# Attention with a distance bias and two feed-forward stages: rows 64 to 191 of the bias built by distance, scores of full pairs from three fp32r products

## The chip, the cores and the metric

One core of a Trainium2 chip. The metric is the device time of one execution in microseconds (us); 585.6 us is the median of three runs of the kernel before (585.51 to 585.66). In this kernel and at this scatter a difference under about 0.2% (1.2 us) can't be told from none.

## The reference

```python
B, H, S, D = 2, 8, 576, 64
scores = q @ k.T / 8
x = log1p(|i - j|) / log1p(max(i, 1))
bias = relu(x * w1 + b1) @ w2                  # 32 hidden units, 8 heads
attn = softmax(scores + bias) @ v              # then 1152 tokens x 512
h = x @ w_in;   g = P(h) / Q(h);  y = g @ w_out      # 512 -> 2048 -> 512, rational function
h = y @ w2_in;  z = piecewise quadratic of h;  out = z @ w2_out
```

The bias depends on the row i and on the distance |i - j|. All is fp32.

## The kernel before, in words

**Order.** Every operation of the attention stage is registered under a kind and a number (`op`, L179), with the letters of the engines that may run it: P TensorE (PE), V VectorE (DVE), A ScalarE (ACT), G GpSimd (POOL), S the DMA queue of SyncE (SP). The table `PLAN` (L34) gives each a position and one letter; `run` (L769) sorts the positions and issues in that order. Each engine works through its own instructions in this order, so an instruction that waits holds back all behind it on its engine. The first steps of the feed-forward stage (`gen`) and the splits of its first weights (`w00` to `w14`, six of the input and seven of the output weights) stand in the same table; the rest of that stage follows in its own loop (`moe`, L624).

**Bias** (`bias_rows`, L251). 36 blocks of 16 rows. A block has four `relu` (L271 to L274, 128 partitions = 4 rows x 32 units), matmuls against w2 (`mm`, L285), a scaled eviction from PSUM (`bev`, L288) and a `st` store. Blocks 0 to 11 (rows 0 to 191) are "near": all 576 columns, each half in its own PSUM bank (or, for those in `one`, both halves in one double bank), stored into an SBUF tile `bias0`. Later blocks are functions of the distance: they compute only max(576 - i0, i0 + 16) distances, mirror the rest (`mir`, L300), go to DRAM (`bd`), and a load per unit and head (`lb`, L326) reads each row at its own shift into one of four `bias` tiles. `dup` (L486) copies rows 0 to 63 to the upper partitions.

**Attention** (`attn`, L345). 20 units: five row blocks ("t": rows 0 to 63 of both batches together, then 0 to 3: 128 rows each from row 64) times four head pairs; 36 pairs of work, 4 of "t" and 32 full ones. A pair is scores (`qk`, L372: fp32 matmuls, per 288 columns one on rows 0 to 63 of the array for the even head and one on rows 64 to 127 for the odd), `ttr` (L397, DVE: add the bias, take the row's extreme), `exp` (L402, ACT, with row sum), `eps` (L406: add 1e-9 to two sums), `rec` (L410), `norm` (L213), nine transposes (`tr`, L431), three evictions (`tev`), 20 matmuls with V (`pv`, L446), and `xh`/`xl` (L463, L465), which split the result into an fp32r part and an fp32r remainder for the next stage. K stays in SBUF as fp32 (`lk`, L489), Q is loaded per unit (`lq`).

**Feed-forward.** Each product is three fp32r matmuls (high x high, high x low, low x high; L714 and L757), 12 of 384 columns per step; ACT, DVE and POOL do the functions between.

Of the kernel before, what the change touches and what calls it, by code (L numbers as in the profile page):

```python
# [31 lines left out]
PAR = {'pb': 4, 'ptb': 3, 'ahead': 2, 'hid': 9, 'bbuf': 6, 'drg': 1.764, 'vb': 4, 'hb': 4, 'qb': 4, 'gb': 11, 'lag': 9, 'shift': 3, 'inb': 4, 'outb': 3, 'c2': 2, 'c3': 1, 's0': [1, 1, 2, 3, 4, 4], 's1': [1, 2, 3], 'mp': 4.15, 'cw': [10, 12, 14, 16], 'cl': [[0, 3, 6, 9], [5, 8, 11, 14]], 'bias': 4, 'one': [0, 1, 2, 3, 4, 8, 5, 9], 'early': 8, 'load': [1.69, 1.22, 0.773]}  # L32

PLAN = {  # L34
    'us0': ([0],
# [25 lines left out]
    'exp': ([98, 100, 132, 135, 173, 175, 182, 218, 217, 216, 238, 235, 279, 263, 293, 323, 316, 335, 336, 367, 357, 358, 402, 408, 450, 442, 454, 482, 486, 490, 519, 520, 553, 549, 574, 587, 588, 607, 622, 611, 670, 688, 693, 692, 707, 699, 708, 745, 763, 764, 769, 779, 817, 819, 844, 846, 881, 883, 902, 903, 922, 934, 955, 954, 968, 960, 970, 999, 998, 1003, 1014, 1027],
        'AAAAAAAAAAAAAAAAAAAAAAAAAAAAAAAAAAAAAAAAAAAAAAAAAAAAAAAAAAAAAAAAAAAAAAAA'),
    'eps': ([102, 137, 176, 219, 237, 241, 280, 325, 337, 380, 375, 434, 456, 487, 516, 552, 554, 589, 617, 654, 689, 694, 710, 760, 788, 787, 820, 878, 906, 905, 937, 957, 969, 1001, 1026, 1028],
        'AAAAAAAAAAAAAAAAAAAAAAAAAAAAAAAAAAAA'),
# [2 lines left out]
    'rec': ([120, 159, 185, 231, 239, 244, 300, 332, 347, 381, 379, 438, 468, 492, 517, 556, 559, 602, 618, 659, 690, 701, 738, 762, 789, 808, 826, 888, 907, 913, 941, 958, 983, 1012, 1033, 1029],
        'VVVVVVVVVVVVVVVVVVVVVVVVVVVVVVVVVVVV'),
    'norm': ([147, 146, 165, 164, 189, 188, 236, 247, 254, 252, 255, 253, 301, 303, 350, 345, 365, 364, 383, 382, 426, 425, 440, 461, 470, 471, 496, 502, 530, 528, 561, 558, 581, 560, 605, 604, 627, 661, 668, 669, 721, 718, 720, 719, 765, 739, 773, 771, 803, 798, 827, 828, 850, 851, 889, 891, 908, 910, 914, 929, 946, 976, 959, 971, 987, 1000, 1020, 1019, 1038, 1041, 1042, 1030],
        'GGGGGGAGGGAGGGGVGGGGGVGGVGGAGGGVGGGGGGGGGGGGAVGGGAGGGGGGAVGVVGAVGAGAGAAA'),  # L70
    'mir': ({12: 151, 13: 187, 14: 201, 15: 260, 16: 313, 17: 296, 18: 339, 19: 340, 20: 361, 21: 506, 22: 412, 23: 453, 24: 501, 25: 258, 26: 529, 27: 570, 28: 579, 29: 623, 30: 527, 31: 731, 32: 625, 33: 772, 34: 744, 35: 709},
        'GGGAAGAAAGGAAGGVAAAAGGGA'),
    'tr': ([153, 156, 157, 170, 169, 168, 193, 194, 192, 249, 257, 248, 262, 287, 285, 256, 283, 304, 305, 330, 306, 351, 353, 352, 370, 371, 372, 401, 428, 430, 429, 444, 432, 462, 463, 464, 474, 476, 475, 514, 534, 535, 540, 545, 550, 571, 569, 568, 592, 593, 591, 651, 650, 649, 653, 663, 662, 676, 677, 675, 722, 733, 732, 723, 727, 724, 784, 786, 778, 776, 785, 777, 805, 804, 806, 829, 831, 830, 852, 873, 853, 898, 899, 900, 919, 920, 928, 938, 939, 940, 952, 978, 977, 994, 993, 992, 1007, 1006, 1008, 1023, 1024, 1025, 1046, 1047, 1051, 1048, 1050, 1049],
        'PPPPPPPPPPPPPPPPPPPPPPPPPPPPPPPPPPPPPPPPPPPPPPPPPPPPPPPPPPPPPPPPPPPPPPPPPPPPPPPPPPPPPPPPPPPPPPPPPPPPPPPPPPPP'),
# [2 lines left out]
    'lv': ([197, 198, 202, 200, 204, 203, 270, 268],
        'SSSSSSSS'),
    'pv': ([205, 228, 251, 302, 355, 329, 354, 369, 427, 473, 472, 513, 512, 562, 578, 590, 648, 674, 717, 716, 774, 775, 832, 799, 884, 897, 896, 926, 951, 962, 1004, 1044, 1043, 1045, 1068, 1067],
        'PPPPPPPPPPPPPPPPPPPPPPPPPPPPPPPPPPPP'),  # L80
    'xh': ({0: 240, 2: 277, 4: 317, 6: 326, 8: 377, 10: 447, 12: 489, 14: 526, 16: 597, 18: 687, 20: 697, 22: 780, 24: 792, 25: 847, 26: 849, 27: 818, 28: 904, 29: 909, 30: 935, 31: 975, 32: 991, 34: 1055, 36: 1057, 38: 1079},
# [821 lines left out]
```

## Time and profile before

| | us |
|---|---|
| median of the runs | 585.6 |
| the profiled execution | 586.15 |
| its span, first to last instruction | 584.3 |
| PE busy | 568.4 (97%) |
| DVE busy | 482.1 (83%) |
| ACT busy | 416.0 (71%) |
| POOL busy | 328.6 (56%) |

Rows name line, engine, operation, output<-input. A busy PE may hold several matmuls in flight, so its busy time says that it had work, not that it ran at its peak; the chain of waits says whether others waited for it. PE, LD (PEld, weight loads), DVE, ACT and POOL run side by side. The granted TensorE clock is 1.00 in every stretch, the upper of its two levels (2.4 GHz).

### The profile page before, as it was taken

The numbers are of one execution on the slowest core, as the hardware profiler recorded it, in microseconds if no ns is written. First come the engines' busy times: TensorE is split into PE (matmuls) and PEld (weight loads), VectorE is DVE, ScalarE is ACT, GpSimd is POOL, SyncE is SP. The second block draws the span as 40 slices with busy tenths as digits, with TensorE's granted clock in tenths as the row PEclk, the third lists the DMA queues.
The fourth block names the chain that finished last, engine by engine and source line by source line (L and its number), as shares of the span: only waits on it lengthen the run. The fifth ranks groups of instructions, "written<-read, shape, count | busy, mean of one in ns | idle before, by whom it ended". The sixth has DMA issues, their size and how long they took to land.

```text
span 584.3 us, 11340 instructions
## 1 busy us (share of the span) xinstructions
PE 568.4 (97%) x4164; PEld 514.7 (88%) x4164; DVE 482.1 (83%) x951; ACT 416.0 (71%) x912; POOL 328.6 (56%) x335
## 2 busy tenths in 40 slices
PE   5999999999999899999999999999999999999997
PEld 3466766678788899999999999999999999999997
DVE  6998788889979888989998979999985998784332
ACT  5999999998999988787888788356554554443430
POOL 0343223343358776899998876664761964574220
PEclk9999999999999999999999999999999999999999
DMA  6985545575712112222221212331431222100012
GB/s 222 226 284 168 188 134 189 191 221 186 253 49 108 37 54 92 73 73 81 101 73 72 73 37 72 109 108 38 145 108 37 98 83 73 38 36 1 29 48 88
DMA packets 25288, 62.72 MB, mean 107 GB/s; under 512 B 3601, under 2 KB 7569, under 8 KB 25233
## 3 DMA queue, kind: packets, MB, share of 16 engines
q1 hardware_dynamic: 25088, 61.90, 32.3%
q8 instruction: 33, 0.54, 0.4%
q14 instruction: 23, 0.18, 0.1%
q10 hardware_dynamic: 144, 0.10, 0.1%
HBM read 48.83 MB, written 9.62 MB: 100 GB/s over the span
## 4 chain that ended last, share of the span: by engine, by line
PE 85%; ACT 6%; DVE 6%; issue 2%; DMA 1%; DVEq 0%; ACTq 0%
PE outps L757 31%; PE inps L714 31%; PE vps L446 7%; PE tps L431 6%; PE sps L382 6%; PE bps L285 4%; ACT P L402 1%; ACT hid L272 1%; DVE wc L522 1%; DVE x2l L690 1%; DVE wc L526 1%; DVE hid L274 1%; DMA small<-small 1%; ACT v L581 1%; ACT h L579 1%
## 5 line engine op out<-in xcount | busy, mean ns | idle before, releaser
L757 PE MATMUL outps<-gh,wo 128*128 128x384 f32 x768 | 209.5, 335 | 0.0
L620 POOL TENSOR_TENSOR gl<-v,gh 128x384 fp32r<-128x384 f32 x96 | 110.8, 1155 | 78.6 <-ACT gh L616 74.2
L757 PEld LDWEIGHTS outps<-gh,wo 128*128 128x128 f32 x768 | 139.9, 188 | 0.0
L757 PE MATMUL outps<-gl,wo 128*128 128x384 f32 x384 | 128.3, 334 | 0.0
L714 PE MATMUL inps<-x,wh 128*128 128x384 f32 x384 | 99.0, 338 | 1.8 <-DVE v L612 1.7
L213 POOL TENSOR_SCALAR P<-P,m 128x576 f32<-128x576 f32 x51 | 38.2, 757 | 71.7 <-DVE m L410 60.0
L583 ACT ACTIVATE v<-inps,cst 128x384 f32<-128x384 f32 x48 | 27.8, 579 | 66.5 <-PE inps L714 63.6
L714 PEld LDWEIGHTS inps<-x,wh 128*128 128x128 f32 x384 | 69.0, 188 | 3.8 <-DVE v L612 3.4
L757 PEld LDWEIGHTS outps<-gl,wo 128*128 128x128 f32 x384 | 72.1, 188 | 0.0
L607 DVE SCALAR_TENSOR_TENSOR v<-v 128x384 f32<-128x384 f32 x48 | 39.5, 823 | 34.1 <-ACT v L583 33.9
L714 PE MATMUL inps<-x2l,wh 128*128 128x384 f32 x192 | 64.6, 337 | 1.7 <-DVE x2l L690 1.7
L616 ACT ACTIVATE gh<-v 128x384 fp32r<-128x384 f32 x96 | 50.8, 529 | 20.4 <-DVE v L608 19.3
L714 PE MATMUL inps<-x2h,wh 128*128 128x384 f32 x192 | 64.6, 337 | 0.0
L714 PE MATMUL inps<-x,wl 128*128 128x384 f32 x192 | 64.5, 336 | 0.0
L714 PE MATMUL inps<-x2h,wl 128*128 128x384 f32 x192 | 64.5, 336 | 0.0
L526 DVE SCALAR_TENSOR_TENSOR wc<-raw,wc 128x512 int32<-128x512 int32 x64 | 59.4, 937 | 0.1
L587 POOL TENSOR_TENSOR q<-h,q 128x384 f32<-128x384 f32 x48 | 49.4, 1031 | 16.3 <-ACT q L580 15.9
L397 DVE CUSTOM_DVE_ANT_0 P<-sps,bias 128x576 f32<-128x576 f32 x72 | 51.9, 752 | 7.4 <-PE sps L382 3.4
L402 ACT ACTIVATE P<-P,m 128x576 f32<-128x576 f32 x72 | 55.2, 768 | 2.7 <-DVE m L397 2.7
L579 ACT ACTIVATE h<-inps,sb 128x384 f32<-128x384 f32 x48 | 28.3, 589 | 29.1 <-PE inps L714 29.1
L672 DVE TENSOR_TENSOR acc<-acc,outps 128x384 f32<-128x384 f32 x61 | 33.4, 547 | 18.8 <-PE outps L757 18.8
L446 PEld LDWEIGHTS vps<-PT,V 128*64 128x64 f32 x800 | 39.5, 137 | 7.6 <-issue 4.1
(83 smaller groups left out, 1211.3 us busy)
## 6 DMA issues: line engine op xcount, KB each, us to landing
raw<-w SPq DMA_DIRECT2D x64, 512.0 KB
bd<-bbuf SPq DMA_DIRECT2D x24, 295.5 KB
bias<-bd SPq DMA_DIRECT2D x24, 288.0 KB
bias<-bbuf SPq DMA_DIRECT2D x12, 288.0 KB
V<-v SPq DMA_DIRECT2D x8, 320.0 KB
K<-kc SPq DMA_DIRECT2D x4, 576.0 KB
out<-acc SPq DMA_DIRECT2D x12, 192.0 KB
Q<-qm SPq DMA_DIRECT2D x16, 128.0 KB
```

The lines of the kernel that those rows point to most:

```text
L213: nc.gpsimd.tensor_scalar(out, x, scale, 1.0, ALU.mult, ALU.mult)
L382: PE.matmul(S_[2 * i + e][c:c + w, x, :288], lhsT=Q[n][r, bb, 0:w], rhs=f(K[hp])[r, bb, 288 * x:288 * x + 288], start=True, stop=True, til ...
L397: V.tensor_tensor_reduce(halves(o), S_.pop(t)[:, :, :288], halves(bt), -0.125, 3e38, ALU.add, ALU.min, sums[i][:, 0, e:e + 1])
L402: A.activation(s, s, AF.Exp, bias=m[:, 0, e:e + 1], scale=-1.0, accum_out=m[:, 1, e:e + 1])
L446: PE.matmul(out[64 * e:64 * e + 64], lhsT=Vt[hp][:, bb, j, 64 * e:64 * e + 64], rhs=PT[i][:, (j, 5 + j if j < 4 else 4)[e], c], start=(j = ...
L526: return [(dict(V=0.7), lambda e: V.scalar_tensor_tensor(tc, words[:, :, 0], 29, tc, ALU.logical_shift_right, ALU.bitwise_or))]
L587: return [lambda: G.tensor_tensor(o["q"], o["h2"], o["q"], ALU.add)] if m == 0 else []
L607: return [lambda: V.scalar_tensor_tensor(v, v, 1.0, v, ALU.min, ALU.mult), lambda: V.tensor_tensor(v, v, h2, ALU.add)]
L616: return [lambda: A.activation(gh, o["v"], AF.Copy)]
L620: return [lambda: G.tensor_tensor(gl, o["v"], f(o["gh"]), ALU.subtract)]
L714: nc.tensor.matmul(ps[:, :U], lhsT=w[:, c], rhs=y[:, c], start=(t == 0), stop=(t == 11))
L757: nc.tensor.matmul(ps[:, :U], lhsT=w[:, c], rhs=y, start=(t == 0), stop=(t == 11))
```

## The change

1. Blocks 4 to 11 (rows 64 to 191) become like the later ones: 512 down to 400 distances instead of 576 columns, one bank, a mirror, a store to DRAM, and loads for units 4 to 7 (8 more `lb`, 8 more `mir`, 8 fewer `mm` and 4 fewer `bev`). One `bias0` tile is left, for "t".
2. Full pairs (not "t"): K and Q are split into fp32r high and low parts (`kh`, `kl`, `qh`, `ql`), and scores are the sum of three fp32r products, the two heads in turn. The high and low K parts take all eight slots of the ring in which four K and the first split output weights (`wo`) lay before. Raw K of two head pairs is held in tiles that later take `x`, of the others in the near pool.
3. `eps`, `dup`, `xh` may go to more engines; raw Q has 3 buffers, split Q 3, `hid` 10; the table is new.

Letters of the table that differ (before -> after): relu A 61, V 83 -> A 71, V 73; bev A 25, V 19 -> A 23, V 17; mir A 12, G 11, V 1 -> A 7, G 20, V 5; eps A 36 -> A 15, V 7, G 14; xh A 24 -> A 9, V 15; tev A 59, V 49 -> A 68, V 40; norm A 12, V 9, G 51 -> A 9, V 10, G 53; w03 A 1, V 2, G 3 -> V 1, G 5; w04 G 6 -> V 4, G 2; w13 V 2, G 5 -> A 1, V 1, G 5; w14 V 3, G 4 -> V 4, G 3. New: kh A 2, V 1, G 1; kl V 3, G 1; qh A 7, G 8, V 1; ql V 2, G 14. Of these, kh of head pairs 0 to 2, kl of 0 to 2, qh and ql of the first unit and the mirrors of blocks 4 to 11 stand ahead of the `ttr` of the first full pair.

```diff
-PAR = {... 'hid': 9, ... 'one': [0, 1, 2, 3, 4, 8, 5, 9], ...}
+PAR = {... 'hid': 10, 'q': 3, 'qs': 3, ... 'one': [0, 1, 2, 3], ...}
...
 def near_row(pr, m):
-    return 64 * (pr // 4) + pr % 4 + 4 * m
+    return pr + 4 * m
...
-        near = pr < 12
+        near = pr < 4
...
-                b = 64 * (pr >= 8)
-                nc.sync.dma_start(self.bias0[pr >= 4][b + pr % 4:b + 64:4], st["buf"][:, 0:S])
+                nc.sync.dma_start(self.bias0[pr:64:4], st["buf"][:, 0:S])
...
+        def split_q(e, n, low):
+            if low:
+                Ql[n] = self.slot(pq, "Ql", cfg["qs"], [128, B, 128], F32R)
+                self.sub(e, Ql[n], Q[n], f(Qh[n]))
+            else:
+                Qh[n] = self.slot(pq, "Qh", cfg["qs"], [128, B, 128], F32R)
+                self.copy(e, Qh[n], Q[n])
+
+        def load_k(hp):
+            K[hp] = f(self.xs0(hp, "Kx")[:, 0:3]).rearrange("p a c -> p (a c)") if hp < 2 else self.kn[hp - 2]
+            nc.sync.dma_start(K[hp], a["kc"][hp])
+
+        def split_k(e, hp, low):
+            x = K[hp]
+            if low:
+                Kl[hp] = self.ring("Kl")
+                self.sub(e, Kl[hp], x, f(Kh[hp]))
+            else:
+                Kh[hp] = self.ring("Kh")
+                self.copy(e, Kh[hp], x)
...
-                        PE.matmul(S_[2 * i + e][c:c + w, x, :288], lhsT=Q[n][r, bb, 0:w],
-                                  rhs=f(K[hp])[r, bb, 288 * x:288 * x + 288], start=True, stop=True,
-                                  tile_position=(64 * e, c))
+                    for m, (q, y) in enumerate(((Qh[n], Kh[hp]), (Qh[n], Kl[hp]), (Ql[n], Kh[hp]))):
+                        for e in range(2):
+                            r = slice(64 * e, 64 * e + 64)
+                            PE.matmul(S_[2 * i + e][c:c + w, x, :288], lhsT=q[r, bb, 0:w], rhs=y[r, k],
+                                      start=m == 0, stop=m == 2, tile_position=(64 * e, c))
...
-                bt = self.bias0[bk == 0][:, h] if bk in (0, "t") else bias[n, e][:]
+                bt = self.bias0[:, h] if bk == "t" else bias[n][:, e]
...
-            bias[n, e] = self.load_bias(pq, bk, h, cfg["bias"])
+            if n not in bias:
+                bias[n] = self.slot(pq, "bias", 2, [128, B, S])
+            self.load_bias(bias[n][:, e], bk, h)
...
-            for e in range(2) if n >= 8 else ():
+            if n >= 4:
+                op("qh", n, "VAG", lambda e, n=n: split_q(e, n, 0))
+                op("ql", n, "VG", lambda e, n=n: split_q(e, n, 1))
+            for e in range(2) if n >= 4 else ():
```

## Rows read from the trace of the kernel before

**Rows 1.** Windows: us, busy of PE, PEld, DVE, ACT, POOL (instructions), clock, DMA

```profile
15.00:45.00 30.00, 29.31 (x373) 15.77 (x367) 28.49 (x76) 29.66 (x68) 12.93 (x20) 1.00 0.86 246
45.00:142.00 97.00, 96.48 (x1068) 68.08 (x1063) 83.60 (x236) 92.56 (x239) 33.78 (x49) 1.00 0.57 187
142.00:197.00 55.00, 53.08 (x469) 45.33 (x468) 48.54 (x112) 51.10 (x120) 31.74 (x34) 1.00 0.36 119
5.00:45.00 40.00, 37.13 (x453) 20.64 (x455) 37.69 (x98) 37.05 (x78) 12.93 (x20) 1.00 0.84 250
```

**Rows 2.** Chain of waits: start, us, what; one full pair, the ramp, feed-forward

```profile
58.44 1.17 PE sps L382 x8
59.61 1.13 PE tps L431 x9
...
188.31 0.47 ACT q L580
...
197.59 2.09 PE outps L757 x12
...
300.06 2.08 PE inps L714 x12
```

**Rows 3.** Timeline of PE and PEld in one pair's scores: start, us, engine, line

```profile
130.73 0.41 PE L382 MATMUL sps<-K,Q 64*128 64x288 f32 x2
130.73 0.19 PEld L382 LDWEIGHTS sps<-K,Q 64*128 64x128 f32 x2
130.97 0.41 PE L382 MATMUL sps<-K,Q 64*128 64x288 f32 x2
```

**Rows 4.** Groups by line and form, PE: busy us, mean ns | idle before

```profile
L285 PE MATMUL bps<-hid,w2s 128*32 128x288 f32 x208 | 17.2, 451 | 7.7 <-DVE hid L274 6.6 <-ACT bbuf L201 0.7
...
L285 PE MATMUL bps<-hid,w2s 128*32 128x512 f32 x8 | 1.0, 592 | 0.0
...
L285 PE MATMUL bps<-hid,w2s 128*32 128x400 f32 x8 | 0.9, 511 | 0.0
```

**Rows 5.** Groups by line and form, ACT

```profile
L272 ACT ACTIVATE hid<-us,thr 128x576 f32<-128x576 f32 x15 | 11.1, 770 | 3.4 <-DVE thr L243 3.0 <-PE bps L285 0.3
L406 ACT ACTIVATE m<-m,cst 128x2 f32<-128x2 f32 x36 | 10.2, 289 | 0.3
...
L463 ACT ACTIVATE x<-vps 128x256 fp32r<-128x256 f32 x12 | 4.5, 376 | 0.1
...
L201 ACT ACTIVATE bbuf<-bps,small 128x288 f32<-128x288 f32 x4 | 1.9, 485 | 0.0
...
L201 ACT ACTIVATE wh<-wc 128x512 fp32r<-128x512 f32 x2 | 1.3, 630 | 0.0
...
L201 ACT ACTIVATE bbuf<-bps,small 128x448 f32<-128x448 f32 x1 | 0.6, 623 | 0.0
```

**Rows 6.** Groups by line and form, DVE

```profile
L205 DVE COPY PT<-tps 128x384 f32<-128x384 f32 x49 | 26.1, 549 | 6.7 <-PE tps L431 6.4
L274 DVE TENSOR_SCALAR hid<-us,thr 128x576 f32<-128x576 f32 x33 | 15.5, 529 | 0.9 <-PE bps L285 0.7
...
L216 DVE TENSOR_TENSOR wl<-wc,wh 128x512 fp32r<-128x512 f32 x5 | 5.0, 1009 | 0.0
...
L205 DVE CAST wh<-wc 128x512 fp32r<-128x512 f32 x7 | 5.0, 709 | 0.0
...
L274 DVE TENSOR_SCALAR hid<-u,thr 128x464 f32<-128x464 f32 x2 | 0.9, 446 | 0.0
```

**Rows 7.** Groups by line and form, POOL

```profile
L216 POOL TENSOR_TENSOR wl<-wc,wh 128x512 fp32r<-128x512 f32 x27 | 38.2, 1418 | 6.1 <-DVE wh L205 3.2 <-ACT wh L201 2.9
...
L211 POOL TENSOR_SCALAR wh<-wc 128x512 fp32r<-128x512 f32 x23 | 15.5, 674 | 25.1 <-PE inps L714 22.7 <-DVE wc L526 2.5
```

**Rows 8.** Timeline of DVE and POOL while POOL was idle, early

```profile
10.59 7.18 DVE L274 TENSOR_SCALAR hid<-us,thr 128x576 f32<-128x576 f32 x16 [0.44 <-PE bps L285]
...
19.51 2.94 POOL L486 COPY bias<-bias 64x576 f32<-64x576 f32 x4 [18.58 <-DMA bias<-bbuf]
```

More of the change, by code (lines that the diff above doesn't have):

```diff
@@ L29, in f @@
     return ap.bitcast(F32)
-PAR = {'pb': 4, 'ptb': 3, 'ahead': 2, 'hid': 9, 'bbuf': 6, 'drg': 1.764, 'vb': 4, 'hb': 4, 'qb': 4, 'gb': 11, 'lag': 9, 'shift': 3, 'inb': 4, 'outb': 3, 'c2': 2, 'c3': 1, 's0': [1, 1, 2, 3, 4, 4], 's1': [1, 2, 3], 'mp': 4.15, 'cw': [10, 12, 14, 16], 'cl': [[0, 3, 6, 9], [5, 8, 11, 14]], 'bias': 4, 'one': [0, 1, 2, 3, 4, 8, 5, 9], 'early': 8, 'load': [1.69, 1.22, 0.773]}
+PAR = {'pb': 4, 'ptb': 3, 'ahead': 2, 'hid': 10, 'q': 3, 'qs': 3, 'bbuf': 6, 'drg': 1.764, 'vb': 4, 'hb': 4, 'qb': 4, 'gb': 11, 'lag': 9, 'shift': 3, 'inb': 4, 'outb': 3, 'c2': 2, 'c3': 1, 's0': [1, 1, 2, 3, 4, 4], 's1': [1, 2, 3], 'mp': 4.15, 'cw': [10, 12, 14, 16], 'cl': [[0, 3, 6, 9], [5, 8, 11, 14]], 'bias': 4, 'one': [0, 1, 2, 3], 'early': 8, 'load': [1.69, 1.22, 0.773]}
@@ L61 @@
[L61 to L64, printed above, removed]
@@ L65 @@
-    'late': ([110],
-        'S'),
[L67 to L74, printed above, removed]
@@ L77 @@
[L77 to L81, printed above, removed]
-        'AAAAAAAAAAAAAAAAAAAAAAAA'),
@@ L91 @@
-    'w00': ([455, 596, 705, 797, 836, 1031],
-        'AAAAAA'),
-    'w01': ([478, 615, 740, 807, 842, 1058],
-        'VVVVVV'),
-    'w02': ([481, 619, 758, 887, 894, 1060],
-        'VVVVVV'),
-    'ab': ([504],
-        'S'),
-    'w03': ([533, 626, 770, 890, 924, 1061],
-        'VGVGAG'),
-    'w04': ([580, 796, 795, 1040, 925, 1086],
-        'GGGGGG'),
-    'bias_end': ([813],
-        '-'),
-    'lw1': ([814, 815, 855, 859, 862, 867, 869, 870, 871],
-        'SSSSSSSSS'),
-    'w10': ([837, 848, 916, 948, 1002, 1063, 1064],
-        'AAAAAAA'),
@@ L109 @@
[L109 to L119 removed]
+    'kh': ([122, 18, 63, 291],
+        'AVAG'),
+    'ql': ({4: 19, 5: 234, 6: 300, 7: 337, 8: 430, 9: 490, 10: 529, 11: 538, 12: 612, 13: 686, 14: 744, 15: 791, 16: 857, 17: 932, 18: 949, 19: 984},
+        'VGGGGGGGGGVGGGGG'),
@@ new lines @@
+    'lv': ([164, 165, 212, 214, 213, 61, 219, 221],
+        'SSSSSSSS'),
+    'mir': ({4: 64, 5: 123, 6: 113, 7: 111, 8: 76, 9: 115, 10: 112, 11: 128, 12: 247, 13: 281, 14: 184, 15: 270, 16: 266, 17: 323, 18: 338, 19: 359, 20: 364, 21: 482, 22: 489, 23: 546, 24: 532, 25: 297, 26: 533, 27: 610, 28: 611, 29: 695, 30: 552, 31: 761, 32: 746, 33: 788, 34: 805, 35: 745},
+        'AAGGVGGAAAGGGGGVGGGAGGGGGGVVGGAV'),
+    'dup': ([72, 91, 110, 108, 107, 109, 114, 160],
+        'GGGGGGGG'),
+    'qk': ([89, 103, 138, 157, 167, 228, 255, 277, 308, 328, 352, 391, 447, 471, 505, 510, 540, 562, 589, 628, 666, 698, 707, 711, 758, 782, 840, 847, 888, 914, 944, 947, 985, 990, 1007, 1044],
+        'PPPPPPPPPPPPPPPPPPPPPPPPPPPPPPPPPPPP'),
@@ new lines @@
+    'ttr': ([92, 93, 116, 117, 139, 140, 168, 169, 207, 211, 237, 238, 260, 267, 285, 301, 311, 325, 341, 342, 370, 396, 424, 425, 454, 455, 474, 476, 511, 512, 516, 517, 569, 570, 590, 591, 602, 603, 655, 656, 681, 688, 713, 714, 727, 734, 739, 740, 766, 768, 828, 829, 841, 842, 870, 871, 910, 912, 923, 924, 952, 959, 967, 968, 991, 992, 1008, 1010, 1034, 1038, 1045, 1046],
+        'VVVVVVVVVVVVVVVVVVVVVVVVVVVVVVVVVVVVVVVVVVVVVVVVVVVVVVVVVVVVVVVVVVVVVVVV'),
+    'kl': ([145, 194, 118, 320],
+        'VVVG'),
@@ new lines @@
+    'exp': ([120, 126, 127, 148, 154, 189, 197, 196, 208, 244, 264, 249, 274, 279, 332, 333, 335, 334, 373, 395, 381, 408, 436, 438, 466, 468, 475, 488, 521, 523, 534, 551, 596, 572, 608, 615, 625, 677, 670, 674, 691, 722, 730, 726, 728, 756, 748, 773, 811, 830, 853, 849, 863, 864, 879, 874, 920, 925, 941, 940, 961, 960, 974, 975, 994, 998, 1014, 1029, 1047, 1048, 1064, 1063],
+        'AAAAAAAAAAAAAAAAAAAAAAAAAAAAAAAAAAAAAAAAAAAAAAAAAAAAAAAAAAAAAAAAAAAAAAAA'),
+    'eps': ([147, 150, 195, 224, 245, 265, 296, 339, 344, 405, 417, 439, 469, 492, 530, 581, 609, 620, 678, 683, 733, 749, 783, 774, 833, 856, 868, 887, 938, 942, 962, 976, 1015, 1050, 1049, 1069],
+        'GVAGVGGGAAGVAGGGAVAGVGAVVGAAAAAAAAGG'),
@@ new lines @@
+    'rec': ([149, 175, 199, 236, 250, 268, 307, 360, 346, 406, 419, 444, 486, 514, 553, 582, 622, 654, 689, 684, 736, 760, 787, 812, 835, 859, 882, 911, 953, 964, 969, 996, 1018, 1051, 1052, 1071],
+        'VVVVVVVVVVVVVVVVVVVVVVVVVVVVVVVVVVVV'),
+    'norm': ([162, 161, 182, 183, 225, 231, 252, 253, 259, 258, 269, 302, 319, 318, 362, 361, 363, 358, 421, 410, 431, 420, 484, 481, 491, 493, 531, 528, 554, 555, 585, 584, 649, 650, 661, 662, 690, 697, 687, 696, 750, 747, 770, 775, 789, 790, 815, 813, 836, 855, 872, 869, 883, 931, 926, 922, 955, 954, 971, 970, 983, 982, 1002, 1000, 1028, 1023, 1058, 1060, 1097, 1084, 1073, 1083],
+        'GGGGGGGGGGVVGGGGGVGAGGGGGGGGGGGGGGGGAGGGGGVAGGVGGGGAVGGGGVGGGGVAAAVVAAGG'),
@@ new lines @@
+    'tev': ([185, 186, 190, 205, 210, 209, 227, 242, 239, 271, 273, 287, 278, 292, 289, 294, 324, 340, 374, 376, 387, 403, 404, 418, 412, 423, 434, 437, 443, 464, 467, 470, 504, 518, 535, 519, 515, 545, 544, 565, 568, 598, 567, 595, 574, 613, 614, 653, 664, 665, 671, 692, 694, 712, 716, 719, 717, 701, 718, 702, 755, 765, 763, 818, 819, 820, 848, 850, 851, 827, 854, 860, 861, 880, 878, 886, 918, 915, 916, 937, 950, 929, 930, 939, 973, 980, 978, 993, 999, 997, 1001, 1019, 1016, 1022, 1024, 1025, 1066, 1067, 1082, 1086, 1104, 1089, 1107, 1108, 1111, 1085, 1110, 1112],
+        'VVAAAAAVVVVAAAAAVVAAVAAVAVVVAVAAAAAAVAAAVAAAVAAVVVAVVVVAVAVAAVVAAAAAAAVVVAAVAAVAAAAAAVAAAVAVAAAAAAAAVVVVAAAA'),
@@ new lines @@
+    'xl': ({0: 235, 2: 283, 4: 306, 6: 399, 8: 398, 10: 433, 12: 526, 14: 593, 16: 658, 18: 715, 20: 764, 22: 831, 24: 858, 25: 884, 26: 936, 27: 917, 28: 966, 29: 1011, 30: 1021, 31: 1020, 32: 1080, 34: 1081, 36: 1123, 38: 1124},
+        'VVVVVVVVVVVVVVVVVVVVVVVV'),
+    'near_end': ([331],
+        '-'),
+    'lw0': ([413, 415, 502, 638, 643, 895, 903, 904],
+        'SSSSSSSS'),
+    'w00': ([414, 441, 597, 723, 810, 1065],
+        'AAAAAA'),
+    'w01': ([440, 485, 619, 771, 908, 1102],
+        'VVVVVV'),
@@ new lines @@
+    'w02': ([445, 487, 663, 832, 909, 1103],
+        'VVVVVV'),
+    'w03': ([480, 741, 743, 834, 921, 1118],
+        'GGGVGG'),
+    'ab': ([539],
+        'S'),
+    'w04': ([573, 742, 769, 881, 951, 1126],
+        'VGVVVG'),
+    'bias_end': ([809],
+        '-'),
+    'lw1': ([817, 825, 896, 898, 900, 901, 902, 905, 906],
+        'SSSSSSSSS'),
+    'w10': ([867, 943, 1017, 1026, 1056, 1068, 1096],
+        'AAAAAAA'),
+    'w11': ([907, 965, 1027, 1039, 1057, 1088, 1099],
+        'VVVVVVV'),
@@ L120 @@
+    'w12': ([963, 979, 1030, 1040, 1059, 1098, 1101],
+        'VVVVVVV'),
+    'w13': ([1031, 1032, 1036, 1062, 1070, 1109, 1125],
+        'GGGGVAG'),
+    'w14': ([1035, 1033, 1037, 1087, 1100, 1127, 1129],
+        'GVVVVGG'),
+    'moe_end': ([1074],
+        '-'),
+    'gen': ([1075, 1076, 1094, 1116, 1117, 1119, 1120, 1128],
         '--------'),
@@ L222, in bias_consts @@
         self.u = p.tile([128, S], F32, name="u")
-        self.us = near.tile([128, 764], F32, name="us")
+        self.us = near.tile([128, 628], F32, name="us")
         small = p.tile([128, 194], F32, name="small")
         wcol, blk, psi, self.rpsi = small[:, 0:10], small[:, 10:14], small[:, 14:158], small[:, 158:194]
-        for c in (slice(128, 764), slice(0, 128)):
-            nc.sync.dma_start(self.us[:, c], a["lskew"][:, c])
+        nc.sync.dma_start(self.us, a["lskew"])
         nc.scalar.dma_start(small, a["small"])
@@ L240, in w2s @@
                 w.rearrange("p (o h) -> p o h", o=1).to_broadcast([128, 4, 8]), ALU.mult)
-        scale_us(slice(128, 764))
+        nc.vector.tensor_scalar(self.us, self.us, wcol[:, 0:1], None, ALU.mult)
         nc.vector.tensor_scalar(self.thr, psi, wcol[:, 1:2], None, ALU.mult)
         self.op("w2s", 0, "V", w2s)
-        self.op("us0", 0, "V", lambda: scale_us(slice(0, 128)))
-        self.bias0 = [near.tile([128, H, S], F32, name=f"bias0{i}") for i in range(2)]
+        self.bias0 = near.tile([128, H, S], F32, name="bias00")
+        self.kn = [near.tile([128, B * S], F32, name=f"Kn{i}") for i in range(2)]
         self.op("lu", 0, "S", lambda: nc.sync.dma_start(self.u, a["ltab"]))
@@ L324, in bias_rows, with load_bias @@
         op("st", pr, "S", store)
-    def load_bias(self, pool, bk, h, bufs):
+    def load_bias(self, t, bk, h):
         nc = self.nc
-        t = self.slot(pool, "bias", bufs, [128, S])
         bd = self.bd[bk][:]
@@ L348, in attn @@
         halves = lambda z: z.rearrange("p (x c) -> p x c", x=2)
-        K = [self.ring(f"K{h}").rearrange("p (b s) -> p b s", b=B) for h in range(H // 2)]
+        K, Kh, Kl, Qh, Ql = {}, {}, {}, {}, {}
         Vt = [p.tile([128, B, 5, 128], F32, name=f"V{h}") for h in range(4)]
-        self.K = K
         units = [(bk, hp) for bk in ("t", 0, 1, 2, 3) for hp in range(4)]
@@ L379, in qk @@
                     w, c = (128, 0) if bk != "t" else (64, 64 * bb)
-                    for e in range(2):
-                        r = slice(64 * e, 64 * e + 64)
-                        PE.matmul(S_[2 * i + e][c:c + w, x, :288], lhsT=Q[n][r, bb, 0:w],
-                                  rhs=f(K[hp])[r, bb, 288 * x:288 * x + 288], start=True, stop=True,
-                                  tile_position=(64 * e, c))
+                    k = slice(S * bb + 288 * x, S * bb + 288 * x + 288)
+                    if bk == "t":
+                        for e in range(2):
+                            r = slice(64 * e, 64 * e + 64)
+                            PE.matmul(S_[2 * i + e][c:c + w, x, :288], lhsT=Q[n][r, bb, 0:w], rhs=K[hp][r, k],
+                                      start=True, stop=True, tile_position=(64 * e, c))
+                        continue
+                    for m, (q, y) in enumerate(((Qh[n], Kh[hp]), (Qh[n], Kl[hp]), (Ql[n], Kh[hp]))):
+                        for e in range(2):
+                            r = slice(64 * e, 64 * e + 64)
+                            PE.matmul(S_[2 * i + e][c:c + w, x, :288], lhsT=q[r, bb, 0:w], rhs=y[r, k],
+                                      start=m == 0, stop=m == 2, tile_position=(64 * e, c))
         def tile_(t):
@@ L402, in exp, with eps @@
                 A.activation(s, s, AF.Exp, bias=m[:, 0, e:e + 1], scale=-1.0, accum_out=m[:, 1, e:e + 1])
-            def eps():
+            def eps(e_):
                 m = sums[i]
-                A.activation(m[:, 2], m[:, 1], AF.Identity, bias=self.cst[:, 3:4])
+                if e_ == "A":
+                    A.activation(m[:, 2], m[:, 1], AF.Identity, bias=self.cst[:, 3:4])
+                else:
+                    (V if e_ == "V" else self.nc.gpsimd).tensor_scalar(m[:, 2], m[:, 1], 1e-9, 0.0, ALU.add, ALU.add)
             def rec():
@@ L418, in tile_ @@
             if e:
-                op("eps", i, "A", eps)
+                op("eps", i, "AVG", eps)
                 op("rec", i, "V", rec)
@@ L457, in pair_, with out @@
                      2: [(1, 0, 128, 256), (2, 128, 128, 0)], 3: [(2, 0, 256, 128)]}[bk]
-                def out(k, u, c, w, d):
+                def out(e, k, u, c, w, d):
                     src = vps[:, n % 2].rearrange("p b q -> p (b q)")[:, c:c + w]
-                    xh, xl = (x[k][u][:, hp, d:d + w] for k in range(2))
+                    for j in range(2):
+                        if x[j][u] is None:
+                            x[j][u] = self.xs0(j, f"x{j}")
+                    xh, xl = (x[j][u][:, hp, d:d + w] for j in range(2))
                     if k == 0:
-                        A.activation(xh, src, AF.Copy)
+                        self.copy(e, xh, src)
                     else:
@@ L772, in run @@
         self.xp = [self.pool(ctx, "xp")]
-        bigt = lambda name, u: self.xp[u > 0].tile([128, 4, U], F32R, tag="big", name=name, bufs=4 if u else 2)
-        x = [[bigt(f"x{i}", 0), None, None] for i in range(2)]
+        self.xs0 = lambda i, name: self.xp[0].tile([128, 4, U], F32R, tag=f"big{i}", name=name, bufs=1)
+        turn = iter(range(6))
+        bigt = lambda name, u: self.xp[1].tile([128, 4, U], F32R, tag="big", name=name, bufs=4) if u else self.xs0(next(turn) % 2, name)
+        x = [[None] * 3, [None] * 3]
         self.wq = [dict(loaded=0, split=0) for _ in range(2)]
@@ L873, in layout @@
     blk = np.repeat(np.eye(4, dtype=np.float32), 32, axis=0)
-    row = np.array([[near_row(pr, m) if pr < 12 else 16 * pr + m for m in range(16)] for pr in range(36)])
+    row = np.array([[near_row(pr, m) if pr < 4 else 16 * pr + m for m in range(16)] for pr in range(36)])
     rows = np.repeat(psi[row].reshape(144, 4).T, 32, axis=0)
```

93 lines of the change are left out of this document (41 added, 52 removed).

## The prediction

> **What bounds the kernel now.** I read the windows first, then the chain of waits, then single instructions. From 197 us on the feed-forward stage runs on PE without gaps, and the change leaves it alone: what can move is the time at which attention hands over. The windows show three stretches of attention [rows 1]. From 5 to 45 us ACT and DVE are full (37.1 and 37.7 of 40 us; from 15 us on 29.7 and 28.5 of 30). From 45 to 142 us PE is full (96.5 of 97), but ACT has 92.6 and DVE 83.6: PE leads them only by a little. From 142 to 197 us all three are near full. POOL alone has room, 78.5 of 192 us busy (12.9, 33.8 and 31.7). The chain says the same [rows 2]: in the middle it goes from PE group to PE group (a pair's scores 1.17 us, its transposes 1.13), and in the ramp up to 197 us it lies on ACT's functions.
>
> **The scores.** A matmul's record in fp32 comes twice, so a full pair has 8 records, two side by side on the two halves of the array. Two starts are 130.73 and 130.97 [rows 3], 0.243 us for two records and four such rounds a pair, 0.97 us; weight loads of 0.19 us start with the round before and are hidden. The rest of 1.17 us is the first load and the switch to half-array tiles, which stay. After, a pair has 12 records of one pass, six rounds. The price of a round isn't shown: no fp32r matmul runs on half the array. The nearest rows are the feed-forward ones: a step of 12 takes 2.08 us [rows 2], 0.173 for 384 columns, which for 288 columns is 0.130; half of the fp32 round (two passes) is 0.122. I take 0.133, as some of 0.173 may be fixed: 6 x 0.133 = 0.80, a gain of 0.17 a pair, **5.4 us** for 32. Ends: 0.122 a round gives 7.7 us of gain; 0.173, if a round can't be shorter than the shortest fp32r step that the rows show, gives 1.04 a pair, 2.2 us of loss.
>
> That rests on the hidden weight load. The Trainium skill (TensorE: Matmul & The Clock Gate, part 3, "The mechanism") says that a weight load overlaps matmuls in flight only where its row group differs, and that a load takes columns / 1.2 ns. The trace disagrees: in [rows 3] two loads start at 130.73 with the matmuls of their own halves in flight, and the next round comes 0.24 us later, no more. By that rule the sum would be another; it is a rival below.
>
> **Bias matmuls.** A near block has 16 records of 288 columns at 17.2 / 208 = 0.083 us, 1.3 us; a shorter one 8, from 1.0 (512) to 0.9 us (400) [rows 4]. Eight blocks: 10.6 down to 7.7 us, 2.9 us less. They lie in the first stretch, where PE waits for others: I count nothing for them, since ACT and DVE cover.
>
> **The work around it,** by letters of the table times durations of rows (K parts have 1152 elements, 2.25 times the 512 of a weight's rows; Q parts 256, half).
> - ACT: 21 `eps` fewer at 0.289, -6.1; 15 `xh` fewer at up to 0.376, -5; 5 mirrors (under 200 columns, at most like the 256 of `xh`) -1.9; 3 norms like a relu of 576, -2.3; evictions -1.5; 9 `tev` more at some 0.5, +4.5; 10 relus more (0.770 at 576, shorter ones less) +4.9; two `kh` 1.42 each, +2.8; seven `qh` +2.6 [rows 5]. Sum -2.0 us.
> - DVE: `kh` 1.6; three `kl` between 1.6 (cast) and 2.3 (subtraction), taken as 1.8, +5.4; three Q parts +1.2; 15 `xh` +5.3; 7 `eps` +1.2; mirrors +1.5; a norm +0.6; four `w04` at 1.0, +4.0; 9 `tev` fewer at 0.549, -4.9; 10 relus fewer and 16 others shorter (0.529 at 576, 0.446 at 464), -5.7; other weight splits and the second scaling of the table -1.0 [rows 6]. Sum +9.2.
> - POOL: `kl` 3.2, `kh` 1.5, 14 `ql` at 0.71, 8 `qh` at 0.34, 14 `eps` at about 0.2, 9 mirrors, 2 norms and 2 `w03`, less five remainders of weights at 1.42 [rows 7]: about +19, covered by POOL's idle time, 113 us.
>
> **DMA.** Eight stores go to DRAM instead of SBUF, and eight loads of 288 KB are new; lacking a wait for them in the trace, I bound their cost by 0 and 3 us. All 8 blocks must land before the first full `ttr`, and SP, which works in order, holds V and later Q loads behind the first of these loads. In the order table some ten DVE instructions (relus of later blocks, evictions, a `kl`) stand between the last store and that `ttr`, 5 us or more by the rows: I take 0. If it is late, DVE stops and with it the next scores, since the PSUM double banks come free only after `ttr`. The DMA share, 0.86 from 15 to 45 us, is why I keep the 3.
>
> **The splits' places.** `wo` gets ring slots only as the last units' scores end, so its splits move behind them, towards the ramp. They are POOL's and DVE's, while the ramp's chain lies on ACT [rows 2]: 0 taken, 2 us at most.
>
> **The sum by stretches.** First stretch, bound by ACT and DVE: added are `kh` 2.8 + 1.6, `kl` 5.4, the first Q parts 0.8, four mirrors 1.5; gone are 32 x 0.08 us of shorter relus, four times two evictions of 288 for one of about 448 (0.97 against 0.62), the second scaling 0.3, three `eps` 0.9. Net 12.1 - 5.2 = 6.9 us on two engines, 3.4 us each; as the two have 5.3 us idle there, between 0.8 and 3.4, and I take **+2.5**. Middle stretch, bound by PE: 24 of the 32 pairs, 24 x 0.17 = 4.1 us of gain. ACT would then need 91 of 93 us, DVE about 89, 98% and 95%: just what both reached from 15 to 45 us [rows 1]. I take **-3.5**. Last stretch: 8 pairs, 1.4 us, of which ACT's ramp lets through part, **-1.0**. Sum -2.0 us: 586.15 - 2.0 = 584.2 for the profiled execution; that one stands 0.55 above the median of the runs, so **583.6 us**.
>
> **Rivals.**
> - *ACT and DVE take over everywhere (slower).* PE's gain is then worth nothing, and the two engines' net work, +9.2 - 2.0 = 7.2 us, divided over them, adds 3.6 us: 589 us. The point from which it decides is the middle stretch: if DVE can't pass its 83.6 / 97 = 86% there by much. For it speaks that POOL's new work may slow DVE: 16 relus with POOL idle took 7.18 / 16 = 0.449 us each [rows 8], the mean over all is 0.529 [rows 6]. POOL's busy share would go from 41 to some 51%; if the 0.08 us comes from POOL, a quarter more of it, 0.02 us on some 200 DVE instructions, is 4 us more on DVE, and the time about 591. Against it speak 95 and 99% from 15 to 45 us. Chance 0.28. (The Trainium skill, SBUF — State Buffer, has DVE and GpSimd share a port pair as an exclusive lock; the two relu durations agree, but don't prove it.)
> - *PE decides everywhere (faster).* Both PE gains arrive, 5.4 + 2.9 = 8.3 us: 577.3 us. Needs ACT and DVE at 98% all through; chance 0.12.
> - *A round of fp32r costs 0.173.* PE gets 2.2 us more, and nothing comes back: 586 to 589 us. Chance 0.07.
> - *Weight loads don't hide behind matmuls of their own half.* A round is then a load, at most 0.126 us for 128 columns by the transposes (1.13 / 9 each, [rows 2]), and a pass of 0.122: six are 1.49 us against 0.97, and 0.52 x 32 = 17 us more make 602 us. With the page's 107 ns for the load it would be about 13 us more. The loads in [rows 3] speak against it; chance 0.05.
> - *The products are not single-pass on half the array,* each costing what one fp32 product did: 2.9 us a pair, 62 us more, 648 us. Twelve feed-forward matmuls have 12 records [rows 2], so 0.01.
>
> **How the numbers follow.** The forecast has 0.47; its own range is 580.5 to 586 (K's cost in the first stretch, DMA up to 3, middle gain 2 to 4). Of it 0.40 is faster by over 0.2% (1.2 us, about what a measurement tells), 0.07 within. Rival two adds 0.12 to faster; of rival one 0.07 falls within 0.2% and 0.21 beyond; of the third 0.03 and 0.04; the last two 0.06 slower. Faster 0.52, same 0.17, slower 0.31. The range takes in rivals one to three: 577.5 to 590.5; outside are the last two and the edges of one and two, under 0.2.
>
> **What would show it.** Scores of a full pair at about 1.0 us in the chain, starts 0.13 us apart two by two; bias matmuls 2.9 us less; POOL at about 98 us before the hand-over; the first full `ttr` no later than its DVE work allows; the first output matmul of the feed-forward stage at about 195.6 us instead of 197.6 [rows 2]. Wrong is the forecast if a DMA releases that `ttr`, if the chain of the middle goes over DVE or ACT rather than PE, or if a round is 0.17 us or more.

## The result, and the profile after

The changed kernel takes 580.19 us (median of 8 runs, 578.94 to 583.91) against 585.66 us (8 runs, 585.51 to 586.48): ratio 0.9906, 95% interval 0.9892 to 0.9919, so 5.5 us less. The prediction was 583.6 (577.5 to 590.5): the direction and the range hold, but the gain is more than twice the 2.0 us that were summed, and the time lies just below the forecast's own range (580.5 to 586). The profiled execution is the fastest of the eight: 578.94 us, with a span of 577.1.

Windows of the changed kernel, to be laid beside [rows 1] (us; busy PE, PEld, DVE, ACT, POOL with instructions; clock; DMA share; GB/s), and one up to its hand-over, the first output matmul of the feed-forward stage:

```profile
15.00:45.00 30.00, 27.20 (x332) 14.25 (x327) 28.79 (x76) 29.80 (x68) 17.55 (x27) 1.00 0.86 262
45.00:142.00 97.00, 96.83 (x1211) 75.02 (x1205) 89.09 (x258) 93.39 (x232) 55.74 (x88) 1.00 0.65 208
142.00:197.00 55.00, 53.14 (x471) 48.90 (x470) 49.82 (x118) 52.73 (x118) 33.16 (x39) 1.00 0.36 123
5.00:45.00 40.00, 35.72 (x411) 18.85 (x413) 38.40 (x99) 39.77 (x84) 17.55 (x27) 1.00 0.83 255
...
0.00:190.70 190.70, 179.40 (x2045) 136.47 (x2046) 172.58 (x463) 181.09 (x419) 102.00 (x155) 1.00 0.62 198
```

The same window of the kernel before, up to its own hand-over:

```profile
0.00:197.40 197.40, 187.09 (x1980) 134.45 (x1981) 171.00 (x448) 182.39 (x437) 79.25 (x109) 1.00 0.56 179
```

Up to the hand-over PE has 7.7 us less, ACT 1.3 less, DVE 1.6 more, POOL 22.8 more. The chain of waits of the changed kernel (start, us, what):

```profile
31.92 6.60 DMA bias<-bd
38.52 0.02 issue
38.54 0.76 DVE P L423
...
58.17 1.00 PE sps L409 x12
...
190.83 2.09 PE outps L803 x12
```

Its shares by line from 45 to 142 us, and the timeline of DVE at 38.54 us:

```profile
by line: PE tps L460 27.9%; PE vps L475 27.5%; PE sps L409 22.5%; PE bps L287 14.8%; POOL P L219 2.6%; DVE P L423 1.1%; POOL bbuf L217 0.9%; POOL wh L217 0.8%; issue 0.7%; POOL Qh L217 0.4%; DVE wc L568 0.3%; POOL m L435 0.2%; DVE m L423 0.
```

```profile
38.54 0.76 DVE L423 CUSTOM_DVE_ANT_0 P<-sps,bias 128x576 f32<-128x576 f32 x1 [0.59 <-DMA bias<-bd]
```

A pair's scores take 1.00 us instead of 1.17, and the hand-over comes at 190.8 instead of 197.6 [rows 2]: of the 7.2 us between the two profiled executions, 6.8 lie ahead of it. From 45 to 142 us the chain still goes from PE group to PE group, but early a new piece stands in it: the bias of rows 64 to 191 coming back from DRAM, for which DVE waits 0.59 us. The timeline of PE in one pair's scores shows the price of a round:

```profile
104.75 0.29 PE L409 MATMUL sps<-Kl,Qh 64*128 64x288 f32 x2
104.89 0.29 PE L409 MATMUL sps<-Kh,Ql 64*128 64x288 f32 x2
...
105.02 0.29 PE L409 MATMUL sps<-Kh,Qh 64*128 64x288 f32 x2
```

Two matmuls start together, the next two 0.13 us later. Groups by line and form of the new work (busy us, mean ns | idle before):

```profile
L222 DVE TENSOR_TENSOR Kl<-Kx,Kh 128x1152 fp32r<-128x1152 f32 x2 | 2.7, 1346 | 0.0
...
L211 DVE CAST Kh<-Kx 128x1152 fp32r<-128x1152 f32 x1 | 0.8, 760 | 0.0
...
L207 ACT ACTIVATE Kh<-Kn 128x1152 fp32r<-128x1152 f32 x1 | 1.2, 1167 | 0.0
...
L222 POOL TENSOR_TENSOR Ql<-Q,Qh 128x256 fp32r<-128x256 f32 x14 | 10.4, 746 | 0.3
L435 POOL TENSOR_SCALAR m<-m 128x2 f32<-128x2 f32 x14 | 4.9, 352 | 12.3 <-ACT P L428 11.8
```

### The profile page after: what moved, and what is told of

Same layout as the page of the kernel before. It is cut to its first block, busy times and chain, and to the rows that moved or that the text cites. A ratio compares the mean times of both kernels' runs of the same rounds, so it can differ in the third digit from the quotient of the medians.

```text
span 577.1 us, 11498 instructions
## 1 busy us (share of the span) xinstructions
PE 560.7 (97%) x4228; PEld 516.7 (90%) x4228; DVE 484.1 (84%) x966; ACT 414.7 (72%) x894; POOL 350.9 (61%) x381
## 4 chain that ended last, share of the span: by engine, by line
PE 84%; DVE 6%; ACT 5%; DMA 2%; POOL 1%; issue 1%; SPq 0%; POOLq 0%; DVEq 0%
PE outps L803 32%; PE inps L760 31%; PE vps L475 7%; PE tps L460 6%; PE sps L409 5%; PE bps L287 3%; ACT hid L274 2%; DMA bias<-bd 1%; DVE wc L568 1%; ACT bbuf L207 1%; DVE x2l L736 1%; DVE wc L572 1%; DMA bd<-bbuf 1%; DMA small<-small 1%; DVE acc L718 1%
## 5 line engine op out<-in xcount | busy, mean ns | idle before, releaser
L219 POOL TENSOR_SCALAR P<-P,m 128x576 f32<-128x576 f32 x53 | 40.7, 776 | 28.4 <-DVE m L439 18.6
L565 ACT ACTIVATE wc<-raw 128x512 f32<-128x512 f32 x64 | 42.9, 679 | 4.8 <-POOL wo L222 4.7
```

The source lines that it names most:

```text
L219: nc.gpsimd.tensor_scalar(out, x, scale, 1.0, ALU.mult, ALU.mult)
L565: return [(dict(A=0.62), lambda e: A.activation(f(tc), x, AF.Prelu, scale=REBIAS, alpha=NEGATIVE))]
```

## The experiments

Two theories: PE sets the hand-over and the cheaper scores are the gain; or ACT and DVE set it and the new order and the work moved to POOL are. All edits are to the changed kernel.

**e1: scores back to fp32.**

```diff
-                    for m, (q, y) in enumerate(((Qh[n], Kh[hp]), (Qh[n], Kl[hp]), (Ql[n], Kh[hp]))):
-                        for e in range(2):
...
+                    for e in range(2):
+                        PE.matmul(..., lhsT=f(Qh[n])[r, bb, 0:w], rhs=f(Kh[hp])[r, k], start=True, stop=True, ...)
```

> The changed kernel with all its splits and its order, but the scores of a full pair again as two fp32 matmuls per 288 columns, on the high parts of Q and K (the low parts are computed and not used). If PE sets the hand-over in the middle stretch, the pair's scores go back from 0.995 to 1.17 us and the time rises by 32 x 0.175 = 5.6 us, to about 585.8. If ACT and DVE set it and the gain came from the new order, it rises by 2 us at most, to under 582.5.

584.26 us (583.58 to 584.86), between the two expectations: 4.1 us of the 5.6 that PE gives back. PE leads, not by all of its 5.6 us.

**e2: no splits, fp32 scores,** which leaves the bias part and the order.

```diff
-                op("qh", ...); op("ql", ...); op("kh", ...); op("kl", ...)
-            K[hp] = f(self.xs0(hp, "Kx")[:, 0:3])... if hp < 2 else self.kn[hp - 2]
+            K[hp] = f(self.ring("K"))
-'q': 3
+'q': 6
```

> Bias part and order of the changed kernel alone: fp32 scores from raw Q and K, no splits (K in four ring slots, Q in six buffers). If PE sets the hand-over: as e1, 585.8, since the splits (about 6 us on DVE, 5 on ACT, 17 on POOL) lie beside PE; at most 1 us less for the first stretch. If ACT and DVE set it: at least 2 us below the changed kernel or about equal to it, 577 to 580.

586.16 us, with runs from 583.72 to 588.53: less work on three engines than e1, and 1.9 us more time. Its profiled execution (588.5, the slowest of the ten) shows why. Timeline of DVE, then the chain, then windows (columns as above):

```profile
38.06 0.76 DVE L422 CUSTOM_DVE_ANT_0 P<-sps,bias 128x576 f32<-128x576 f32 x1 [3.43 <-DMA bias<-bd]
```

```profile
31.61 8.35 DMA bias<-bd
...
40.81 2.28 PE sps L408 x6
```

```profile
38.00:42.00 4.00, 1.94 (x7) 1.20 (x8) 2.35 (x8) 3.13 (x8) 0.34 (x1) 0.83 0.75 252
42.00:46.00 4.00, 4.00 (x18) 1.60 (x15) 2.92 (x8) 2.83 (x8) 1.14 (x2) 0.50 0.64 226
```

Without the splits DVE comes to the first full pair early and waits 3.4 us for its bias, and 1.2 more at the next; PE, which waits for these `ttr` before its scores (1.0 and 1.2 us), is busy 1.94 of 4 us, and then the granted clock is 0.50, the lower level (1.2 GHz): six records of scores take 2.28 us, where eight take 1.17 at the upper. Both theories missed this. Of the ten executions, the three with a mean granted clock of 0.999 or 1.00 took 583.7 to 584.7 us, the seven with 0.994 to 0.997 took 585.8 to 588.5.

**e3: no low parts,** all three products high by high (scores are then three times the high product).

```diff
+                ((Qh[n], Kh[hp]),) * 3
-                op("ql", ...); op("kl", ...)
```

> The low parts of Q and K are not computed; the three fp32r products are all high by high, so PE's work is that of the changed kernel. DVE has about 5 us less (three remainders of K, two of Q), POOL 13 us less. If PE sets the hand-over: 579.5 to 580.5, unchanged but for up to 0.7 us in the first stretch. If DVE sets it: 3 to 5 us less, 575 to 577.

580.33 us (578.6 to 584.54), unchanged: taking work off DVE and POOL brings nothing. Its profiled execution (584.5, the slowest) has the same kind of wait for the bias (2.8 us) and the same low clock near 42 us as e2's, so part of a gain may be hidden by them; the five executions with a mean clock of 0.999 or 1.00 have a median of 579.95, still unchanged.

**e4: two products.** Leaves out low Q by high K, so scores are those of Q rounded to fp32r.

```diff
-                    ..., (Qh[n], Kl[hp]), (Ql[n], Kh[hp])
+                    ..., (Qh[n], Kl[hp])
```

> The third product (low Q by high K) is left out of the scores, its splits stay. PE has two rounds of 0.132 us fewer in x 32 pairs, 0.264 x 32 = 8.4 us less. If PE still sets the hand-over with room behind it: 572 to 574. If ACT (95% busy before the hand-over) and DVE are next at once: 577 to 580.

575.04 us (574.75 to 576.8), between the two expectations: 5.15 of 8.4 us arrive. Window, then the chain by line from 45 to 142 us:

```profile
45.00:142.00 97.00, 95.36 (x1147) 71.18 (x1142) 91.47 (x268) 95.85 (x240) 58.66 (x92) 1.00 0.68 215
```

```profile
by line: ACT P L428 17.6%; PE vps L475 11.2%; ACT PT L207 11.0%; PE tps L460 8.6%; ACT hid L274 8.2%; DVE P L423 7.3%; issue 5.9%; PE bps L287 5.2%; PE sps L409 4.5%; DVE PT L211 3.9%; POOL P L219 3.0%; ACT bbuf L207 2.2%; ACT wc L565 1.9%;
```

ACT is busy 95.9 of 97 us and its lines lead the chain (some 41% of it, PE's some 30%), where in the changed kernel PE's had 93%: the chain has moved in large part from PE to ACT. That ACT alone is the next bound isn't shown; e9 tries it.

**e5: no round trip.** Units 4 to 7 load an input table; their bias is computed and stored, but not used.

```diff
+        if bk == 0:
+            nc.sync.dma_start(t, self.a["ltab"])
+            return
```

> The bias of rows 64 to 191 is still computed, mirrored and stored, but units 4 to 7 load a table of the input of the same shape instead, so that no load waits for the stores to land. If the round trip through DRAM sets the first full pair in the changed kernel: the scatter (578.9 to 583.9) goes and the median falls by 0.5 to 3 us. If it is hidden there behind the splits: 579.5 to 580.5, as the changed kernel.

578.98 us (578.34 to 580.3): 1.2 us less, which is at the edge of what can be told here, as the two kernels' runs overlap. That the scatter goes isn't shown: of the changed kernel's eight runs only one (583.91) lies above 580.6. With the 0.59 us of DVE's wait it fits that the round trip costs the changed kernel about 1 us.

**e6: `eps` on ACT** (letters of the table only).

```diff
-    'eps': (..., 'GVAGVGGGAAGVAGGGAVAGVGAVVGAAAAAAAAGG'),
+    'eps': (..., 'AAAAAAAAAAAAAAAAAAAAAAAAAAAAAAAAAAAA'),
```

> All 36 additions of 1e-9 on ACT as in the kernel before: ACT gets 21 x 0.29 = 6.1 us more, POOL 4.9 and DVE 1.1 less. If PE sets the hand-over and ACT has its room: 580 to 581.5. If ACT, 95% busy before the hand-over, is as near a bound as PE: 583 to 586.

588.47 us (587.81 to 589.03): 8.3 us more for 6.1 us of work, past both expectations. Yet from 45 to 142 us ACT is no fuller than in the changed kernel (90.6 us busy against 93.4), and PE is busy only 91.4 of 97: the time goes into waits. Some 2 us are lost by the first full pair, whose bias lands at 40.6 us instead of 38.5. The chain then has pieces that weren't there:

```profile
54.98 2.64 POOL Kl L222
...
62.22 6.86 DMA raw<-w
```

From this low part of K it goes on over a mirror on POOL to SP's store, to the weight load queued behind that store, and at 69.1 us to ACT's first step of splitting that weight. So a delay on POOL comes back to ACT through SP's queue; that the later `eps` caused POOL's delay fits, but wasn't separated. Some 4 us more are lost between 107 and 126 us.

**e7: 28 of POOL's instructions on DVE** (`ql` and `eps`, letters only).

```diff
-    'ql': ({...}, 'VGGGGGGGGGVGGGGG'),
+    'ql': ({...}, 'VVVVVVVVVVVVVVVV'),
...
-    'eps': (..., 'GVAGVGGGAAGVAGGGAVAGVGAVVGAAAAAAAAGG'),
+    'eps': (..., 'VVAVVVVVAAVVAVVVAVAVVVAVVVAAAAAAAAVV'),
```

> The 14 low parts of Q and the 14 additions that the changed kernel has on POOL run on DVE: DVE gets 14 x 0.50 + 14 x 0.16 = 9.2 us more (what the prediction had reckoned for the whole change, where 1.6 us were measured), POOL 15 less. If DVE's ledger is what the prediction mis-sized, this takes the expected 2 us of the gain or more: 582 to 586. If DVE has that room: 580 to 581.5.

585.43 us (584.9 to 587.39): 5.2 us more for about 9 us of DVE work. But it isn't the amount of work alone. Timeline of DVE:

```profile
57.14 0.64 DVE L222 TENSOR_TENSOR Ql<-Q,Qh 128x256 fp32r<-128x256 f32 x1 [2.90 <-POOL Qh L217]
```

A low part of Q, now on DVE, waits 2.9 us for POOL's high part, which stands behind POOL's 2.7 us of a low K part; all of DVE's later work waits with it, PE is busy 2.31 of the 4 us from 58 us on, and the granted clock is 0.82 there and 0.75 in the next 4. Of the 6.2 us by which this execution's attention falls behind the changed kernel's, 3.7 arise between the `ttr` at 51.9 and the one at 63.3 us (51.5 and 59.2 in the changed kernel). From 45 to 142 us DVE is busy 88.1 us, no more than in the changed kernel (89.1). So e7 mixes the price of the work with that of a new wait.

**e8: V's loads moved,** to shorten the round trip.

```diff
-    'lv': ([164, 165, 212, 214, 213, 61, 219, 221],
+    'lv': ([57.2, 57.4, 212, 214, 213, 178.5, 219, 221],
...
-    'late': ([163],
+    'late': ([57.1],
```

> Only three positions of the order table change: two loads of V and the load of constants go ahead of the first stores, another load of V behind the first bias loads from DRAM, so that those are not queued behind 0.7 MB. If the round trip is what scatters the first full pair: fewer executions over 581 and a median of 579 to 580. If it is hidden: 580.2, unchanged.

581.6 us (580.29 to 582.85; ratio 0.9919, 0.9901 to 0.9938): no gain. In the chain of its profiled execution (582.85, the slowest) the stores land only at 33.5 us (31.1 in the changed kernel), after POOL's mirrors, and the bias loads follow them. But this kernel is late from the start: the load of raw K stands on its chain up to 8.4 us, with two of V's loads now beside it, and the first `ttr` of all starts at 23.5 us instead of 20.9. So e8 doesn't tell whether V's old place lengthened the round trip.

**e9: e4, without low Q, all high Q on POOL.**

```diff
-                    ..., (Qh[n], Kl[hp]), (Ql[n], Kh[hp])
+                    ..., (Qh[n], Kl[hp])
...
-                op("ql", ...)
-    'qh': (..., 'AGVGGGAAGGAAAAGG'),
+    'qh': (..., 'GGGGGGGGGGGGGGGG'),
```

> The third product (low Q by high K) and the low parts of Q are left out, and all 16 high parts of Q are made on POOL: against e4 (575.0) ACT has 7 x 0.42 = 2.9 us less, DVE 1.4 less, POOL 10.4 less and 2.8 more; PE is the same. If ACT is what holds e4: 572 to 573.8. If something else does (PE's rounds, the fixed order): 574.5 to 575.5.

576.09 us (574.5 to 577.76), no better than e4. Its profiled execution (577.76, the slowest) waits for the bias again (DMA bias<-bd, 7.6 us on the chain up to 40.6 us): lighter engines come earlier to the same wait. Whether ACT's lighter load would pay without it stays open.

**e10: e2 without the round trip** (e5's edit on e2).

> e2 (fp32 scores, no splits) with the bias of rows 64 to 191 loaded from an input table instead of through DRAM; it is computed and stored as before. If e2's scatter (583.7 to 588.5) comes from its first full pair waiting for the round trip and from the clock that falls there: no execution over 585.5 and a median of 582.5 to 584.5, by which the bias part and the order alone would be worth 1 to 3 us. If the splits or the order make the scatter: as e2.

582.18 us (582.1 to 582.62): e2's scatter is gone, so it came from the round trip. The bias part and the order alone are worth 3.5 us when no load waits for a store, a little more than expected. From 27 us on the chain of the first stretch is in large part on PE here:

```profile
27.38 1.87 PE sps L406 x16
29.25 1.52 PE bps L287 x16
```

**e11: e10 with the bias matmuls' columns put back** as matmuls whose result is overwritten.

```diff
+            for j in range(4) if 4 <= pr < 12 else ():
+                nc.tensor.matmul(st[x][32 * j:32 * j + 32, :S - d], lhsT=w2, rhs=hid[j][:, :S - d], ...)
```

> e10 with the columns that the change took from the matmuls of blocks 4 to 11 put back: for each of their four groups one more fp32 matmul of 576 - d columns (64 to 176) ahead of the real one, into the same bank. ACT, DVE, POOL and the DMAs are those of e10 (582.2). If PE's bias matmuls lie under ACT and DVE in the first stretch, as the prediction had it: 582 to 582.6. If they count because PE sets the hand-over from the start: the 2 to 3 us that these columns took (2.9 by the prediction's rows), 584.2 to 585.1.

583.55 us (583.34 to 583.76): 1.4 us, between the two and little more than can be told. In e10's setting, without splits and round trip, the shorter bias matmuls count by about half of what was reckoned for them.

**Taken together,** the medians make a path from before to after: 585.66; bias part and order 582.18 (-3.5, of it 1.4 from the bias matmuls); round trip 586.16 (+4.0); splits 584.26 (-1.9); fp32r scores 580.19 (-4.1). Each step holds in its place on the path: the round trip costs 4.0 without splits and 1.2 at the end. It fits that the splits fill the time in which DVE would wait, since its waits for this bias are 4.6 us in e2's profile, 1.1 in e1's and 0.6 in the changed kernel's. Where the clock fell behind the wait, as in e2's profile, that is part of the 4.0 and of the -1.9: e2's three executions without it have a median of 584.5. (A lower mean clock alone says little: in e1 two executions with 0.996 took no longer than the others.)

e4 beats both kernels (ratio 0.9828, 0.981 to 0.9847, against the kernel before), at the price of Q's rounding in the scores.

## Why the prediction was right or wrong

**Right: the scores.** The round was reckoned at 0.133 us, and two of them take 0.27 (starts 104.75, 104.89 and 105.02), by the estimate that scaled the feed-forward step and allowed for a fixed part. Weight loads hide behind matmuls of their own half: a load takes 0.19 us [rows 3] and a round 0.13. The Trainium skill (TensorE: Matmul & The Clock Gate, part 3, "The mechanism") has a rule that they overlap only across row groups; it doesn't hold here, while the background weight buffer, which the same section names beside it, would fit. The middle and last stretches were to give 3.5 + 1.0 = 4.5 us; from e1 to the changed kernel it is 4.1. The middle's chain lies on PE, as forecast.

**Wrong: the first stretch,** "+2.5" for the bias part and the splits. Timeline of DVE: the 13th and the 59th of the 72 `ttr`, before and after:

```profile
44.55 0.74 DVE L397 CUSTOM_DVE_ANT_0 P<-sps,bias 128x576 f32<-128x576 f32 x1
...
142.16 0.76 DVE L397 CUSTOM_DVE_ANT_0 P<-sps,bias 128x576 f32<-128x576 f32 x1 [0.61 <-PE sps L382]
```

```profile
43.63 0.74 DVE L423 CUSTOM_DVE_ANT_0 P<-sps,bias 128x576 f32<-128x576 f32 x1
...
136.79 0.76 DVE L423 CUSTOM_DVE_ANT_0 P<-sps,bias 128x576 f32<-128x576 f32 x1 [0.57 <-PE sps L409]
```

With the hand-over, 6.8 us earlier, that is -0.9, -4.5 and -1.4 us for the three stretches, where the sum had +2.5, -3.5 and -1.0: most of the error is in the first. (The split is rough, since other work moved between the `ttr` and the profiled execution is 1.25 us below its median.) From the kernel before to e1 (same scores, with bias part, order and splits) the whole time falls by 1.4 us.

Three terms are in it. First, the price of the K parts and the use of idle time: six K parts took 7.3 us on the two engines (a high part 0.76 on DVE and 1.15 to 1.17 on ACT, a low one 1.35 to 1.50), not 9.8, as the rows taken for them were means over the whole kernel. So the net 6.9 us shrink to some 4.4, and ACT and DVE had 5.3 us idle: from 5 to 45 us they are busy 3.4 us more together than before, and the stretch got no longer. Second, "I count nothing for them, since ACT and DVE cover": the bias matmuls gave 1.4 us where that was tried (e11). Third, the remaining 2 us of -3.5 go to the order and the moved work; which of its moves they are wasn't tried.

The ledger of DVE over the whole attention erred the same way: +9.2 reckoned; by the same measure, count times mean of each group up to the hand-over, it is +2.6 (busy time, in which neighbours overlap, +1.6). K and Q parts took 6.2 us and not 8.2, the weight splits 1.6 more and not some 3.3, the relus 6.5 less and not 5.7, mirrors and norms 0.8 more and not 2.1. e7, which adds some 9 us to DVE, ends at 585.4, but its wait for POOL keeps that from showing that the ledger's size decides.

**Half right: the round trip.** It was taken as 0 with 3 as its end; in the changed kernel it costs about 1.2 us (e5) and does release a `ttr` of the first full unit (0.59 us of DVE idle), which the prediction had named as a sign against itself. That it costs so little goes with the splits (4.0 us without them, e2 against e10), which the prediction counted as a price only.

**The rivals.** "ACT and DVE take over" didn't happen, but there is little room before it: in e4 ACT's lines lead the chain after 5 us of gain. e6 and e7, with more work on ACT or DVE, lose their time in waits between engines and don't show those two full. "PE decides everywhere" would have been 577.3; e5, without the round trip, comes within 1.7 us of it.
